# The prologue of a spectral mixing and ReGLU kernel in another order: x first on two queues, tables behind it, filters in halves, batch 1's stage A late

## The chip, the cores and the metric

The kernel runs on one core of a Trainium2 chip. The core has a matrix engine (TensorE, PE in the profile, its weight loads PEld), a vector engine (VectorE, DVE), a scalar engine (ScalarE, ACT), GpSimd (POOL) and a sync engine (SyncE, SP). Each of them takes its instructions strictly from its own list, and they wait for one another through semaphores. DMA transfers are issued from the lists of SP, ScalarE and GpSimd and are carried by 16 DMA engines that all of them share. The metric is the time of one execution on the device in microseconds (us); less is better.

## The reference, cut to what matters

Eight batches of 3008 tokens with 256 features are filtered in the frequency domain, and the result goes through a gated layer of width 1536.

```
x: (8, 3008, 256) float32     filt_r, filt_i: (1505, 256)
w_gate, w_val: (256, 1536)    w_out: (1536, 256)

X = rfft(x, axis=1);  Y = X * (filt_r + 1j * filt_i);  y = irfft(Y, n=3008, axis=1)
y = y.reshape(24064, 256)
out = (maximum(y @ w_gate, 0) * (y @ w_val)) @ w_out
```

## The kernel before, in words

The transform of length 3008 is split as 94 x 32 (`N1`, `N2`) and done with matrix products. For one batch the steps are these.

- **Stage A** multiplies x, with the 94 long axis on the partitions, by a cosine and sine table `WA`. x lies in two tiles `XF[0]` and `XF[1]`, 16 of the 32 positions of the short axis each. `load_x` fills them, a third of the rows per DMA, for column ranges given in units of `q`, a quarter of a tile.
- **Turning**: the result has to have the short axis on the partitions. For batch 0 two VectorE transposes do it in SBUF (`turn_a`, from the tiles `AS` to `AT`). For all other batches stage A's result is written to DRAM (`Abuf`) and read back in another order (`at`).
- **Forward transform** of the short axis with the table `F2` (`fwd`), **product** with the filter tiles `Ftr` and `Fti` (`product`), and **inverse transform** with `I2t` and `I2u` (`inv`). Six pieces i = 0 to 5 make a batch, each with eight matmuls, four products and sixteen matmuls. The result goes to DRAM (`Dbuf`) and is read back as `dC` (`load_d`).
- **Last inverse** (`item_c`, the table `M1`), which gives y transposed for a block of 512 tokens (`yT`).
- **The gated layer** (`gv` and `o_part`): 47 blocks of 12 steps. One step makes 128 columns of gate and value of a block (four matmuls, a ScalarE copy, a VectorE product) and a third of an output tile of the block before.

Batches 1 to 7 are transformed in between the steps of the gated layer; `at_step` holds which piece comes behind which step. Batch 1's `fwd` begins at step 16, that is the fifth step of the second block.

The order of the work is written by hand: each engine's list is the order in which the Python code emits instructions, and a DMA takes its place in the list of the engine that issues it. PSUM banks are handed out in rotation by `bank` and `done`. `hold_gpsimd` makes GpSimd wait for a tile, by copying eight columns of it, so that what it issues behind that comes later.

The change is in the **prologue**, all that stands ahead of the stream of the gated layer (lines 568 to 646), and in three helpers.

- `first_a(p, s, h)` is one item of batch 0's stage A: one matmul of 512 columns and a ScalarE copy. There are 16: p is a quarter of the 32 positions, s half of that quarter, h half of the features. p = 0 and s = 0 reads the first quarter of `XF[0]`.
- `items_a(1)` are the 16 items of batch 1's stage A. Items of c = 0 and 1 are copied mostly by ScalarE, those of c = 2 and 3 by VectorE; each fourth item completes a slab that SP writes to `Abuf`. `first_b(amid)` runs batch 0's six pieces, and calls `amid(i)` behind each piece, which may emit some of these items. Eight of the products of batch 0 run on GpSimd (`POOL_U`), from a copy `xs` that ScalarE makes; the other sixteen run on VectorE.
- `make_back_t` and `make_back_u` compute `I2t` and `I2u` on the chip from `F2` and a permutation in `tabs`; `place_own` copies the last groups and `M1` from `tabs`.
- `load_filters` loads the filters, on GpSimd's queue, for the rows 0 to 31 and 64 to 95. `place_filter(fi, a, half, copy)` copies them to the rows 32 to 63 and 96 to 127, for one half of the 24 groups (`H` = 12), with an engine's copy or with a DMA. Pieces 0 to 2 read the first half, pieces 3 to 5 the second.
- `load_vg` and `load_o` load the weights of the gated layer as bf16 (`WvT`, `WgT`, `WoT`), on GpSimd's queue.
- `warm(n)` emits n matmuls on a tile of ones, whose results are not used.

## Time and profile before

| | us |
|---|---|
| median of 3 runs | 891.37 |
| lowest and highest run | 888.9 and 892.23 |
| span of the profiled execution | 885.7 |
| the median above that span | 5.7 |
| TensorE busy | 872.1 (98%) |
| VectorE busy | 575.7 (65%) |
| ScalarE busy | 495.2 (56%) |
| GpSimd busy | 376.4 (43%) |

The profiled execution's own time is not listed apart from the three runs; what the profile has of it is the span, from the first to the last instruction.

The places in the prologue that the prediction uses, in us from the start of the span:

| | from | to |
|---|---|---|
| batch 0's stage A on TensorE | 7.63 | 22.4 |
| the two transposes on VectorE | 19.62 | 27.96 |
| batch 0's last product on GpSimd | 39.48 | 40.64 |
| the last write to `Dbuf` | 43.28 | 46.63 |
| the read of the first `dC` | 46.80 | 50.35 |
| the gated layer's first matmul | 52.32 | |
| the first matmul that reads `WoT` | 66.87 | |
| batch 1's first `fwd` | 73.14 | |

In the profile's lines a name such as L282 is a line of the kernel, and `psA<-XF,WA` means that psA is written from XF and WA. "xN" counts the instructions that were merged into the line. In brackets stands how long the engine idled ahead of them, and who ended that. SPq and ACTq are DMA issues on these engines' lists. The page's rows of digits show the span in 40 slices of 22 us each: a digit is the busy share in tenths. The chain of waits goes back from the last instruction, at each step to what released it.

### The profile page before, as it was taken

The numbers are of one execution on the slowest core, as the hardware profiler recorded it, in microseconds if no ns is written. First come the engines' busy times: TensorE is split into PE (matmuls) and PEld (weight loads), VectorE is DVE, ScalarE is ACT, GpSimd is POOL, SyncE is SP. The second block draws the span as 40 slices with busy tenths as digits, with TensorE's granted clock in tenths as the row PEclk, the third lists the DMA queues.
The fourth block names the chain that finished last, engine by engine and source line by source line (L and its number), as shares of the span: only waits on it lengthen the run. The fifth ranks groups of instructions, "written<-read, shape, count | busy, mean of one in ns | idle before, by whom it ended". The sixth has DMA issues, their size and how long they took to land.

```text
span 885.7 us, 19147 instructions
## 1 busy us (share of the span) xinstructions
PE 872.1 (98%) x7190; PEld 506.9 (57%) x7190; DVE 575.7 (65%) x875; ACT 495.2 (56%) x882; POOL 376.4 (43%) x375
## 2 busy tenths in 40 slices
PE   8989999999999999999999999999999999999997
PEld 3435655666555665556655665556655666666665
DVE  4866766676666676667765776657766577655553
ACT  5734555556555655556555556555655555555552
POOL 4654796147631667216780186803866000000001
PEclk9999999999999999999999999999999999999999
DMA  9994466533645337533376234663446512421111
GB/s 242 304 221 98 155 142 146 141 117 96 150 133 124 98 101 184 129 98 98 103 179 145 81 111 133 165 125 86 123 132 142 118 46 63 105 56 31 38 34 50
DMA packets 106067, 107.28 MB, mean 121 GB/s; under 512 B 20167, under 2 KB 90087, under 8 KB 105334
## 3 DMA queue, kind: packets, MB, share of 16 engines
q1 hardware_dynamic: 81286, 76.03, 33.5%
q0 software_dynamic: 23792, 29.16, 13.3%
q8 instruction: 57, 0.93, 0.4%
q10 hardware_dynamic: 896, 0.86, 0.3%
q14 instruction: 36, 0.29, 0.1%
HBM read 60.42 MB, written 48.23 MB: 123 GB/s over the span
## 4 chain that ended last, share of the span: by engine, by line
PE 92%; DMA 4%; DVE 1%; ACT 1%; issue 0%; POOL 0%; SPq 0%; ACTq 0%; DVEq 0%
PE psV L509 27%; PE psO L530 27%; PE psG L509 26%; PE psF L353 3%; PE psY L493 2%; PE psD L433 2%; PE psX L396 2%; DMA dC<-Dbuf 2%; DMA WoT<-in_moe_w_out_dram 1%; PE psA L282 1%; DVE AT L291 1%; PE psA L303 1%; PE psJ L565 0%; DMA Dbuf<-dsb 0%; DMA Dbuf<-AS 0%
## 5 line engine op out<-in xcount | busy, mean ns | idle before, releaser
L514 DVE SCALAR_TENSOR_TENSOR prod<-psG,vsb 128x512 bf16<-128x512 f32 x564 | 388.8, 690 | 262.4 <-ACT vsb L512 257.1
L512 ACT CAST vsb<-psV 128x512 bf16<-128x512 f32 x564 | 331.9, 589 | 266.5 <-PE psV L509 179.4
L509 PE MATMUL psV<-yT,WvT 128*128 128x512 bf16 x1128 | 337.6, 380 | 0.6 <-DVE yT L500 0.6
L530 PE MATMUL psO<-WoT,prod 128*128 128x256 bf16 x2256 | 336.7, 273 | 1.1 <-DMA WoT<-in_moe_w_out_dram 1.1
L509 PE MATMUL psG<-yT,WgT 128*128 128x512 bf16 x1128 | 335.8, 379 | 0.2 <-ACT yT L498 0.2
L530 PEld LDWEIGHTS <-prod 128*128 128x128 bf16 x2256 | 220.6, 98 | 144.8 <-issue 1.5
L509 PEld LDWEIGHTS <-WgT 128*128 128x128 bf16 x1128 | 110.1, 98 | 135.6 <-issue 2.5
L509 PEld LDWEIGHTS <-WvT 128*128 128x128 bf16 x1128 | 98.6, 98 | 41.3 <-issue 30.3
L274 POOL CAST scr<-prod 128x8 f32<-128x8 bf16 x24 | 4.5, 189 | 245.0 <-DVE prod L514 245.0
L554 POOL DMA_DIRECT2D out_dram<-osb x5 | 2.6, 536 | 195.7 <-ACT osb L543 195.7
L543 ACT COPY osb<-psO 128x512 f32<-128x512 f32 x92 | 53.9, 586 | 25.9 <-PE psO L530 23.5
L412 DVE TENSOR_TENSOR tt<-psX,Ftr 128x512 bf16<-128x512 f32 x96 | 65.0, 680 | 1.6 <-POOL uu L410 0.6
L339 POOL TENSOR_TENSOR fold<-XP 128x1024 f32<-128x1024 f32 x24 | 56.5, 2354 | 19.9 <-PE psF L353 18.8
L412 DVE TENSOR_TENSOR uu<-psX,Fti 128x512 bf16<-128x512 f32 x88 | 59.8, 680 | 0.0
L326 POOL DMA_DIRECT2D XP<-in_x_dram x96 | 57.6, 603 | 3.0 <-PE psG L509 1.6
L340 POOL TENSOR_TENSOR XP<-XP 128x1024 f32<-128x1024 f32 x24 | 56.3, 2348 | 2.0
L441 ACT CAST dsb<-psD 128x512 bf16<-128x512 f32 x94 | 50.6, 591 | 11.0 <-PE psD L433 11.0
L498 ACT CAST yT<-psY 128x512 bf16<-128x512 f32 x47 | 27.5, 586 | 31.0 <-PE psY L493 30.8
L360 DVE CAST asb<-psF 128x512 bf16<-128x512 f32 x48 | 30.9, 686 | 18.6 <-PE psF L353 18.6
L360 ACT CAST asb<-psF 128x512 bf16<-128x512 f32 x48 | 25.8, 589 | 30.5 <-PE psF L353 30.5
L493 PE MATMUL psY<-M,dC 96*128 96x94 bf16 (+18 forms) x604 | 37.7, 198 | 2.8 <-DMA dC<-Dbuf 2.8
L493 PEld LDWEIGHTS <-dC 96*128 96x128 bf16 x604 | 34.4, 97 | 7.2 <-DMA dC<-Dbuf 3.2
(80 smaller groups left out, 500.9 us busy)
## 6 DMA issues: line engine op xcount, KB each, us to landing
XP<-in_x_dram POOLq DMA_DIRECT2D x48, 256.0 KB, 5.8
Dbuf<-dsb SPq DMA_DIRECT2D x23, 512.0 KB
dC<-Dbuf SPq DMA_DIRECT2D x57, 192.0 KB
XP<-in_x_dram POOLq DMA_DIRECT2D x96, 96.0 KB, 2.6
Abuf<-asb SPq DMA_DIRECT2D x96, 96.0 KB
at<-Abuf SPq DMA_DIRECT2D x24, 384.0 KB
out_dram<-osb SPq DMA_DIRECT2D x69, 94.0 KB
XF<-in_x_dram SPq DMA_DIRECT2D x15, 256.0 KB
```

The source lines that it names most:

```text
L326: nc.gpsimd.dma_start(xp[r:r + 24, 0:4:2, :], _ap(x, (b * N1 * N2 + o) * D, [[N2 * D, 24], [47 * N2 * D, 2], [1, 512]]))
L339: tt(t, xp[:, 0:2], xp[:, 2:4], op=ALU.add)
L340: tt(xp[:, 2:4], xp[:, 0:2], xp[:, 2:4], op=ALU.subtract)
L360: copy(asf[:, :, q, :], banks[q])
L412: nc.vector.tensor_tensor(p, psX, filt, op=ALU.mult)
L441: copy(dsb[:, a, o:o + 2, :], psD[a])
L493: nc.tensor.matmul(psY[:, o:o + w], dCs[b, n2 // 8][:, n2 % 8, h * 128:(h + 1) * 128], M1[:, n1:n1 + w], start=True, stop=True)
L509: nc.tensor.matmul(pt[:, :W], w[:, h, ft * 128:(ft + 1) * 128], yt[:, h, :], start=(h == 0), stop=(h == 1))
L512: nc.scalar.copy(vsb, psV[:, :W])
L514: nc.vector.scalar_tensor_tensor(prod, in0=psG[:, :W], scalar=0.0, in1=vsb, op0=ALU.max, op1=ALU.mult)
L530: nc.tensor.matmul(psO[:, t % 2], prods[ft][:, t * 128:(t + 1) * 128], WoT[:, ft, :], start=(ft == 0), stop=(ft == NFT - 1))
L543: copy(osb[:, t0 % 2:t % 2 + 1], psO[:, t0 % 2:t % 2 + 1])
```

## The change

The prologue's instructions are put in another order and on other queues.

- x of batch 0 is loaded ahead of the tables, its first two quarters on the queues of SP and ScalarE in turn. The first quarter is loaded in four parts (the fourth fills the partitions that are otherwise zeroed), so that it needs no memset. `F2` and `tabs` come behind x, on SP.
- Stage A of batch 0 comes first on TensorE, all of it, and `make_back_t`, `make_back_u` behind it; the copies of `make_back_t` move from VectorE to ScalarE. `place_own` comes behind the transposes.
- The filters are loaded in two halves of the groups, 16 DMAs in place of 8, all behind the fourth piece of x. Three of the four copies of the first half and all of the second are DMAs of SP.
- Batch 1's x comes later on SP. Of the 16 items of batch 1's stage A, three are emitted within batch 0's pieces (before: eight), ten ahead of the first `item_c` and three behind it.
- The first half of the gate and value weights is loaded behind piece 3, the second half at once when the first `dC` is there; then the next `dC`, `WoT`, the other `dC`, and `at` last. Both DMAs of the first `dC` are issued by ScalarE.
- There are fewer warm-up matmuls ahead of the pieces, and two behind each of the pieces 0 to 3.

```diff
-    def load_x(b, eng, cols):
+    def load_x(b, engs, cols, ms=range(3)):
         w = NX2 * D
         for c, c0, c1 in cols:
-            for m in range(3):
+            for m in ms:
                 rows = min(32, B * N1 - (b * N1 + 32 * m))
-                eng.dma_start(XF[c][m:m + 4 * rows - 3:4, c0:c1],
+                engs[m % len(engs)].dma_start(XF[c][m:m + 4 * rows - 3:4, c0:c1],
...
         for e in range(2):
-            nc.vector.tensor_copy(I2t[:, 8 * q + e:8 * q + 8:2, :], psI[e])
+            nc.scalar.copy(I2t[:, 8 * q + e:8 * q + 8:2, :], psI[e])
...
     def load_filters():
-        for src, dst in FILT:
-            for a in range(2):
-                r, k1, n = a * 64, 1 + 24 * a, NG - 2 * a
-                nc.gpsimd.dma_start(dst[r:r + 31:2, 0:n, :], ...
-                yield
-                nc.gpsimd.dma_start(dst[r + 1:r + 32:2, 0:n, :], ...
+        for g0 in (0, H):
+            for src, dst in FILT:
+                for a in range(2):
+                    r, k1, n = a * 64, 1 + 24 * a + g0, H - (2 * a if g0 else 0)
+                    nc.gpsimd.dma_start(dst[r:r + 31:2, g0:g0 + n, :], ...
+                    nc.gpsimd.dma_start(dst[r + 1:r + 32:2, g0:g0 + n, :], ...
+            yield
...
     q = NX2 * D // 4
+    both, sp = (nc.sync, nc.scalar), (nc.sync,)
     nc.sync.dma_start(WA, ...)
-    nc.scalar.dma_start(F2, ...)
-    nc.scalar.dma_start(tabs, ...)
-    filters = load_filters()
-    next(filters)
-    nc.vector.memset(XF[0][:, 0:q], 0.0)
-    nc.gpsimd.memset(XF[0][:, q:2 * q], 0.0)
+    load_x(0, both, ((0, 0, q),), range(4))
     nc.vector.memset(junk, 1.0)
-    nc.vector.memset(XF[0][:, 2 * q:3 * q], 0.0)
-    nc.gpsimd.memset(XF[0][:, 3 * q:], 0.0)
+    nc.vector.memset(XF[0][:, q:2 * q], 0.0)
+    nc.gpsimd.memset(XF[0][:, 2 * q:], 0.0)
     nc.vector.memset(XF[1][:, 0:2 * q], 0.0)
     nc.gpsimd.memset(XF[1][:, 2 * q:], 0.0)
-    load_x(0, nc.sync, ((0, 0, q), (0, q, 2 * q), (0, 2 * q, 4 * q), (1, 0, 2 * q), (1, 2 * q, 4 * q)))
+    load_x(0, both, ((0, q, 2 * q),))
+    load_x(0, sp, ((0, 2 * q, 4 * q), (1, 0, 2 * q), (1, 2 * q, 4 * q)))
+    nc.sync.dma_start(F2, ...)
+    nc.sync.dma_start(tabs, ...)
     for (src, dst) in FILT:
         nc.vector.memset(dst[64:128, NG - 2:, :], 0.0)
+    filters = load_filters()
+    hold_gpsimd(XF[1][:, 2 * q - 8:2 * q])
+    next(filters)
     load_own_filters()
-    hold_gpsimd(XF[0][:, 4 * q - 8:4 * q])
-    for _ in filters:
-        pass
-    warm(8)
+    next(filters)
+    warm(6)
+    for p, s, h in [(p, s, h) for p in range(2) for s in range(2) for h in range(2)]:
+        first_a(p, s, h)
+    for p, h in ((2, 0), (3, 0), (2, 1), (3, 1)):
+        for s in range(2):
+            first_a(p, s, h)
     for i in range(3):
         make_back_t(i)
-    warm(3)
-    for s in range(2):
-        for h in range(2):
-            first_a(0, s, h)
     for i in range(3):
         make_back_u(i)
-    for p, h in ((1, 0), (1, 1), (2, 0), (3, 0), (2, 1), (3, 1)):
-        for s in range(2):
-            first_a(p, s, h)
-    place_own()
     for h in range(2):
         turn_a(h)
-    for i in range(12):
+    place_own()
+    for i in range(6):
         warm(2)
     place_filter(1, 0, 0, nc.gpsimd.tensor_copy)
-    place_filter(1, 1, 0, nc.scalar.copy)
-    for half, cols in ((0, ((0, 0, 2 * q),)), (1, ((0, 2 * q, 4 * q),))):
+    for a in range(2):
+        place_filter(0, a, 0, nc.sync.dma_start)
+    place_filter(1, 1, 0, nc.sync.dma_start)
+    load_x(1, sp, ((0, 0, 2 * q),))
+    for fi in range(2):
         for a in range(2):
-            place_filter(0, a, half, nc.sync.dma_start)
-        load_x(1, nc.sync, cols)
-    for a in range(2):
-        place_filter(1, a, 1, nc.sync.dma_start)
-    load_x(1, nc.sync, ((1, 0, 4 * q),))
-    nc.sync.dma_start(WF, ...)
+            place_filter(fi, a, 1, nc.sync.dma_start)
+    load_x(1, sp, ((0, 2 * q, 4 * q),))
     early = items_a(1)
     def amid(i):
         if i == 3:
             place_nyq()
-        if i == 0:
-            warm(4, 256)
-        for _ in range((0, 1, 1, 2, 2, 2, 0)[i]):
+            load_vg(0, DFF // 2)
+        if i == 3:
+            load_x(1, sp, ((1, 0, 4 * q),))
+        if i < 4:
+            warm(2)
+        for _ in range((0, 0, 0, 0, 1, 1, 1)[i]):
             next(early)()
-    hold_gpsimd(AT[0:32, NG - 1, D - 8:])
-    load_vg(0, DFF // 2)
     first_b(amid)
-    load_d(0, 0, 1, (nc.sync, nc.scalar))
+    load_d(0, 0, 1, (nc.scalar, nc.scalar))
     hold_gpsimd(dCs[0, 0][:, 7, D - 8:])
-    load_vg(DFF // 2, 3 * DFF // 4)
+    load_vg(DFF // 2, DFF)
     load_d(0, 1, 2, (nc.gpsimd, nc.gpsimd))
-    load_vg(3 * DFF // 4, DFF)
+    load_o()
+    load_d(0, 2, 4, (nc.gpsimd, nc.gpsimd))
+    nc.sync.dma_start(WF, ...)
     for i, f in enumerate(early):
         f()
-        if i == 6:
+        if i == 9:
             for h in range(2):
                 item_c(0, h)
-    for c in range(2):
+    for c in range(4):
         load_at(1, c)
-    hold_gpsimd(yTs[0][:, 0, 0:8])
-    load_o()
-    for c in range(2, 4):
-        load_at(1, c)
-    load_d(0, 2, 4, (nc.gpsimd, nc.gpsimd))
```

More of the change, by code (lines that the diff above doesn't have):

```diff
@@ L231, in load_filters @@
     def load_filters():
-        for src, dst in FILT:
-            for a in range(2):
-                r, k1, n = a * 64, 1 + 24 * a, NG - 2 * a
-                nc.gpsimd.dma_start(dst[r:r + 31:2, 0:n, :],
-                                    _ap(src, k1 * D, [[N1 * D, 16], [1, n * D]]))
-                yield
-                nc.gpsimd.dma_start(dst[r + 1:r + 32:2, 0:n, :],
-                                    _ap(src, (N1 - k1) * D, [[N1 * D, 16], [-D, n], [1, D]]))
+        for g0 in (0, H):
+            for src, dst in FILT:
+                for a in range(2):
+                    r, k1, n = a * 64, 1 + 24 * a + g0, H - (2 * a if g0 else 0)
+                    nc.gpsimd.dma_start(dst[r:r + 31:2, g0:g0 + n, :],
+                                        _ap(src, k1 * D, [[N1 * D, 16], [1, n * D]]))
+                    nc.gpsimd.dma_start(dst[r + 1:r + 32:2, g0:g0 + n, :],
+                                        _ap(src, (N1 - k1) * D, [[N1 * D, 16], [-D, n], [1, D]]))
+            yield
     def load_own_filters():
@@ L568 @@
     q = NX2 * D // 4
+    both, sp = (nc.sync, nc.scalar), (nc.sync,)
     nc.sync.dma_start(WA, nc.inline_tensor(wa_h, name="dft_wa").ap())
-    nc.scalar.dma_start(F2, nc.inline_tensor(f2_h, name="dft_f2").ap())
-    nc.scalar.dma_start(tabs, nc.inline_tensor(tab_h, name="dft_tab").ap())
-    filters = load_filters()
-    next(filters)
-    nc.vector.memset(XF[0][:, 0:q], 0.0)
-    nc.gpsimd.memset(XF[0][:, q:2 * q], 0.0)
+    load_x(0, both, ((0, 0, q),), range(4))
     nc.vector.memset(junk, 1.0)
-    nc.vector.memset(XF[0][:, 2 * q:3 * q], 0.0)
@@ L578 @@
-    nc.gpsimd.memset(XF[0][:, 3 * q:], 0.0)
+    nc.vector.memset(XF[0][:, q:2 * q], 0.0)
+    nc.gpsimd.memset(XF[0][:, 2 * q:], 0.0)
     nc.vector.memset(XF[1][:, 0:2 * q], 0.0)
     nc.gpsimd.memset(XF[1][:, 2 * q:], 0.0)
-    load_x(0, nc.sync, ((0, 0, q), (0, q, 2 * q), (0, 2 * q, 4 * q), (1, 0, 2 * q), (1, 2 * q, 4 * q)))
+    load_x(0, both, ((0, q, 2 * q),))
+    load_x(0, sp, ((0, 2 * q, 4 * q), (1, 0, 2 * q), (1, 2 * q, 4 * q)))
+    nc.sync.dma_start(F2, nc.inline_tensor(f2_h, name="dft_f2").ap())
@@ L582 @@
+    nc.sync.dma_start(tabs, nc.inline_tensor(tab_h, name="dft_tab").ap())
     for (src, dst) in FILT:
         nc.vector.memset(dst[64:128, NG - 2:, :], 0.0)
+    filters = load_filters()
+    hold_gpsimd(XF[1][:, 2 * q - 8:2 * q])
+    next(filters)
     load_own_filters()
-    hold_gpsimd(XF[0][:, 4 * q - 8:4 * q])
-    for _ in filters:
-        pass
-    warm(8)
+    next(filters)
+    warm(6)
+    for p, s, h in [(p, s, h) for p in range(2) for s in range(2) for h in range(2)]:
+        first_a(p, s, h)
@@ L605 @@
+    for i in range(6):
         warm(2)
     place_filter(1, 0, 0, nc.gpsimd.tensor_copy)
-    place_filter(1, 1, 0, nc.scalar.copy)
-    for half, cols in ((0, ((0, 0, 2 * q),)), (1, ((0, 2 * q, 4 * q),))):
-        for a in range(2):
-            place_filter(0, a, half, nc.sync.dma_start)
-        load_x(1, nc.sync, cols)
-    for a in range(2):
-        place_filter(1, a, 1, nc.sync.dma_start)
-    load_x(1, nc.sync, ((1, 0, 4 * q),))
-    nc.sync.dma_start(WF, nc.inline_tensor(fold_h, name="dft_fold").ap())
+    for a in range(2):
+        place_filter(0, a, 0, nc.sync.dma_start)
@@ L621, in amid @@
             place_nyq()
-        if i == 0:
-            warm(4, 256)
-        for _ in range((0, 1, 1, 2, 2, 2, 0)[i]):
+            load_vg(0, DFF // 2)
[4 more added lines that the diff above has]
+        for _ in range((0, 0, 0, 0, 1, 1, 1)[i]):
             next(early)()
-    hold_gpsimd(AT[0:32, NG - 1, D - 8:])
-    load_vg(0, DFF // 2)
     first_b(amid)
-    load_d(0, 0, 1, (nc.sync, nc.scalar))
+    load_d(0, 0, 1, (nc.scalar, nc.scalar))
     hold_gpsimd(dCs[0, 0][:, 7, D - 8:])
-    load_vg(DFF // 2, 3 * DFF // 4)
+    load_vg(DFF // 2, DFF)
     load_d(0, 1, 2, (nc.gpsimd, nc.gpsimd))
-    load_vg(3 * DFF // 4, DFF)
+    load_o()
+    load_d(0, 2, 4, (nc.gpsimd, nc.gpsimd))
+    nc.sync.dma_start(WF, nc.inline_tensor(fold_h, name="dft_fold").ap())
     for i, f in enumerate(early):
         f()
-        if i == 6:
+        if i == 9:
             for h in range(2):
                 item_c(0, h)
-    for c in range(2):
+    for c in range(4):
         load_at(1, c)
-    hold_gpsimd(yTs[0][:, 0, 0:8])
-    load_o()
-    for c in range(2, 4):
-        load_at(1, c)
-    load_d(0, 2, 4, (nc.gpsimd, nc.gpsimd))
     prologue.close()
```

## The prediction

> **What bounds the kernel now.** I read the page first, for the whole span.
>
> ```profile
> span 885.7 us, 19147 instructions
> ...
> PE   8989999999999999999999999999999999999997
> ...
> DMA  9994466533645337533376234663446512421111
> ```
>
> TensorE is busy nearly throughout; from the fourth slice on (about 73 us) only work taken off it would pay, and the change takes none off there. What it can win lies in the first three slices, where the DMA engines are full too. So next the chain of waits over the first 75 us, with the steps that carry it.
>
> ```profile
> 2.53 3.60 PE psJ L565 x8
> ...
> 7.79 3.43 PE psA L282 x8
> ...
> 11.88 7.10 PE psA L282 x16
> ...
> 19.62 3.50 DVE AT L291
> ...
> 23.78 4.19 DVE AT L291
> ...
> 43.28 3.35 DMA Dbuf<-AS
> ...
> 46.80 3.55 DMA dC<-Dbuf
> ...
> 52.53 0.85 PE psV L509 x2
> ...
> 57.47 11.43 DMA WoT<-in_moe_w_out_dram
> ...
> 73.21 0.34 PE psX L396 x8
> ```
>
> Each line is start, length, what. Batch 0 goes: warm-up matmuls, stage A (psA), two transposes on VectorE (AT), products and inverse until 43.28, a write to DRAM, the read back (dC), then the gate/value stream (psV). The stream waits once for WoT. The psX at 73.14 in TensorE's timeline (batch 1's first transform, step 16 of the stream) is my finish line: behind it both kernels do the same.
>
> Then the timelines of TensorE, GpSimd and SP, for what each step costs and what it waits for.
>
> ```profile
> 22.23 5.34 PE L565 MATMUL psJ<-junk 128*128 128x512 bf16 x24
> ...
> 41.90 6.25 PE L303 MATMUL psA<-XF,WA 128*96 128x512 f32 x14
> 50.49 0.62 PE L493 MATMUL psY<-M,dC 96*128 96x94 bf16 x12 [2.35 <-DMA dC<-Dbuf]
> ```
>
> ```profile
> 29.77 6.73 POOL L410 TENSOR_TENSOR uu<-xs,Fti 128x512 bf16<-128x512 f32 x6
> 36.57 0.39 POOL L258 COPY Ftr<-nyq 1x256 bf16<-1x256 bf16 x1
> ```
>
> ```profile
> 1.96 10.16 SPq L190 DMA_DIRECT2D XF<-in_x_dram  x15
> ```
>
> Seven batch-1 items cover the trip through DRAM until 48.14, then TensorE idles 2.35 us; and the first matmul pairs of the stream take 0.85 us where later ones take 0.43. Last, the DMA queues between 30 and 43 us:
>
> ```profile
> DMA packets 1504, 4.15 MB, mean 319 GB/s; under 512 B 178, under 2 KB 818, under 8 KB 1395
> ```
>
> That is the rate a full mix of x loads, weights and writes reaches here.
>
> **The change, part by part.**
>
> *Start.* The junk memset leads on VectorE (0.48, ends 1.50 instead of 2.47), and six warm-ups of 3.60/8 = 0.45 end at 4.26. psA then needs the weight table and the first quarter of x: five DMAs on two queues (SP's x issue costs 10.16/15 = 0.68) are issued by 2.5; between the 2.2 us to landing of the 16 KB filter row and the page's 2.6 for a 96 KB x load they are in at 4.0 to 4.9. I take 4.3 for the first psA, against 7.79. The make_back work (0.90 + 0.65 on the chain) is out of the way. But the first warm-ups run at 0.45, the 24 later ones at 5.34/24 = 0.22, and the slow stretch lasted from 2.53 to about 7.0, 4.5 us. Begun at 1.56 it ends at 6.1, so 1.8 us of stage A run at half speed: 0.9 lost; bounds 0 (it ends at 4.3) and 2.1 (it lasts to 8.5, psA's half speed being all of the excess).
> [...]
> From first psA to the twelfth copy the trace has 19.60 − 7.79 = 11.81, less 0.65 of make_back: 11.16. AT starts at 4.3 + 11.16 + 0.9 = 16.4 and ends 8.35 later at 24.7 instead of 27.97: 3.3 gained.
>
> *x in time?* Fifteen x loads at 0.64 to 0.68 on SP would be as slow as before; four of the first seven stay on SP, so the last is issued at 9.4 instead of 12.1, and stage A wants it at 12.9. Free. The extra fourth part (128 KB) and the late tables (wanted by make_back at 19, issued at 10) hide under stage A. [...]
>
> *make_back behind stage A.* Six psI copies move to ScalarE: 0.35 each (VectorE's 2.08/6) to 0.59 (ScalarE's 128x512): 2.1 to 3.5, plus 1.57 for I2u, behind the last AS copy at 19.6: done at 23.3 to 24.7, under the transposes. Without that cover each us would delay the first inverse. place_own (3 × 0.19) now stands ahead of VectorE's first product, which idled 0.50 there for psX: 0.1. Warm-up matmuls removed and added fill waits: free.
>
> *Filters.* GpSimd is held until the fourth chunk of x lands (some 10.5, before 11.81), then issues 16 + 4 DMAs at 0.48 to 0.61: until 21.5. Its Fti copy (2.73), queued behind, ends at 24.3, ahead of its first product at 24.7 + 1.1 = 25.8. SP's three copies of half 0 land before that too. The second half goes through 20 to 27, its copies are issued to 27.5; nothing shows how long SP's copies take, the loads in the same crowd took 5.1 to 6.9, so 32. VectorE wants them at 30.4, GpSimd at 31.7: some 0 to 2 us, mostly under GpSimd's chain; I take 0.
>
> *Products.* Batch 1's items leave this stage (8 before, 3 now), so TensorE is not full here. But GpSimd is: 6.73 for six products, 0.75 for the Nyquist rows, two weight loads now in the middle (0.73 + 0.71), two products at 1.15: 12.0 from 25.8 is 37.8 less overlaps of the copies, say 37.2. Before, the last ended at 40.64, 12.67 after AT; now 12.5. The lighter TensorE buys almost nothing. Inverse and copy take 1.1 to 2.6 (40.64 to 43.28 before, an item's copy in the way); I take 1.6: the last Dbuf write is issued at 38.8 instead of 43.28, 4.5 earlier.
>
> *The write and the read back.* Here the gain is lost again. In before the last x load (28.75) and the first weights (28.26) were through at about 41 and the final write met a free DMA. Now x waits on SP behind the first Dbuf write: that came 7.5 after AT, now at most, so 31.6 to 32.2; the weights follow at 33.5. From 33 on there stand 1.57 MB of Dbuf, 1.57 of x, 0.79 of weights: 3.93 MB at 319 GB/s = 12.3 us, that is 45.3. Bounds: the write overtakes (38.8 + 3.35 = 42.1), or it comes all last with its own latency (47). I take 45.2, nearest to the rate of the same mix, against 46.63. dC now has both issues on ScalarE, one 0.34 after the other, then 3.69: psY at 49.3, before 50.49. Behind the waiting issues ScalarE holds four psA copies; TensorE needs the first of those banks only for the last item before psY, so this adds 0 to 0.5, inside the wait for dC.
> Ten items (0.893 each) now end at 37.7 + 8.9 = 46.6: TensorE still idles some 2.7 us. Behind psY come 0.62 and three items, 2.7: the stream starts at 52.6, before 52.32.
>
> *The stream to the finish line.* Before: 73.14 − 52.32 = 20.8. Clean it would be 17 gate/value steps of 0.865, five outputs of 0.435 and 0.5 of psY: 17.4. Lost are 1.2 to half speed in the first pairs, 1.4 to the two waits for WoT, 0.8 to small waits. WoT is now issued at 52.6 behind weights and one dC (1.97 MB with itself; the queue ran 4.7 MB in 19.4 us from 52.2 on): about 61, wanted at 64: the 1.4 goes. Late next is at: now last of 4.7 MB, 51 + 19.4 = 70.4, wanted at 70.8 to 72. The half speed stays if 2.7 us idle act as 2.35 did; 0 to 1.7 in all, half in my sum. So the finish line: 52.6 + 20.8 − 1.4 − 0.5 = 71.5, a gain of 1.6. The fold table (64 KB, first wanted past 140 us) is off the path.
>
> **Sum.** 885.7 − 1.6 = 884.1 of span. The median of the runs lies 5.7 above the profiled span (the lowest run 3.2), which I carry over: 889.8.
>
> **Rivals.**
> A, *no collision* (25 in 100). The last write gets through by 42.1 because the engines serve SP's queue ahead of GpSimd's. Then psY is bound by the ten items at 46.6, no idle, no half speed: stream at 49.9, finish line 49.9 + 20.8 − 2.6 = 68.1, 5.0 gained, or 3 if at is then late by 2: 886.4 to 888.4, and 885 if the slow start costs nothing. For it: separate queues, and x (SP) is issued ahead of the weights. Against: the DMA engines are busy nearly without a break from 30 to 43.
> B, *slower: the second filter half is late* (15 in 100). The eight small loads may cost as much each as the large ones (seven landed about 1.0 apart, 17 to 22.4, by GpSimd's wait at 21.71). Then half 1 lands at 30 to 32, its copies at 36, and GpSimd's sixth product waits from 31.7: 4 to 5 us straight down the chain to the dC read, 893 to 896. It decides from about 33.5; beyond 38 the kernel is slower by more than 0.5%.
> C, *at is the new stall* (included in the forecast's upper end). at stands last now; if it lands at 73 instead of 70.4 the whole gain goes: 891 to 892.
>
> **How the numbers follow.** Forecast (collision as summed, with C) 60 in 100, its own range 887.5 to 892; A 25, B 15. About 0.5% (4.5 us) is what a measurement of this kernel can tell from no change. Faster than 886.9 is 17 of A's 25, and 7 of the forecast's 60 for bounds that all fall well: 0.24. Slower than 895.8 is the far half of B, 8, and 6 of the forecast where C costs more than its price: 0.14. Within: 0.62. The range takes in A's middle and B's middle: 885.5 to 894.5.
>
> **What would show it.** First psA near 4.3 and at half speed for a while; AT done at 24 to 25.5; GpSimd's last product near 37; the final Dbuf write issued near 39 but landing after 44; TensorE idle for dC again; no wait for WoT, perhaps one for at. I am wrong upward if the write lands at 42 and the stream starts at 50; wrong downward if products wait for Ftr or Fti copies near 31.

## The result and the profile after

| | median, us | runs | lowest and highest |
|---|---|---|---|
| before | 890.37 | 4 | 888.9 to 892.23 |
| after | 900.15 | 4 | 898.09 to 901.15 |

The ratio is 1.0102, with a 95% interval of 1.008 to 1.0124. The change makes the kernel 1.0% slower, 9.8 us; the prediction was 1.6 us faster. The profiled execution of after took 901.15, with a span of 899.4; against the span of before (885.7, an execution at the lower end) that is 13.7 more. The marks that are compared below stand in both in the same order, so the place where the time is lost can be read; the size is that of the medians.

These are the page's span and rows of digits after (40 slices of 22.5 us), and the row of the granted clock before.

```profile
span 899.4 us, 19131 instructions
...
PE   8788999999999999999999999999999999999997
...
PEclk9889999999999999999999999999999999999999
DMA  8897448443465344663355433753346512231111
```

```profile
PEclk9999999999999999999999999999999999999999
```

Nearly all that differs lies in the first four slices: TensorE's digits fall to 7 and 8, and the granted clock to 8. At the gated layer's products 11.9 of the 13.7 have come by 95 us; the other 1.9 are two later waits of TensorE, 1.51 for `dC` at 148.88 (before 0.45) and 0.55 for `at` at 188.51. Next the chain of waits after, from 5 to 84 us, the answer to the chain shown in the prediction (start, length, what).

```profile
5.16 12.37 PE psA L283 x24
...
18.17 3.47 DVE AT L292
...
22.33 4.22 DVE AT L292
26.59 6.91 DMA Ftr<-Ftr
...
34.01 2.57 DMA Fti<-Fti
...
46.40 0.51 SPq L445
...
47.69 6.08 DMA Abuf<-asb
53.81 3.27 DMA dC<-Dbuf
...
57.66 7.21 DMA WvT<-in_moe_w_val_dram
...
74.54 8.65 DMA at<-Abuf
...
83.32 0.41 PE psX L397 x8
```

Three transfers stand here that were not in the chain before: a filter copy (`Ftr<-Ftr`, `Fti<-Fti`), the weights `WvT`, and `at`. The write of batch 0 was there with 3.35 and has become a slow stretch up to 53.8: the profile names `Abuf<-asb`, which landed at 53.77, but the `dC` issue began at 53.40, right behind the last `Dbuf` write's landing at 53.30. The finish line (batch 1's first psX) moves from 73.14 to 83.32, 10.2 later. TensorE's timeline says what each costs there; the brackets hold the idle time ahead and who ended it.

```profile
37.45 0.42 PE L434 MATMUL psD<-tt,I2t 64*64 64x256 bf16 x2 [4.26 <-DVE uu L413]
...
57.21 1.01 PE L494 MATMUL psY<-M,dC 96*128 96x94 bf16 x12 [1.15 <-DMA dC<-Dbuf]
58.05 5.42 PE L304 MATMUL psA<-XF,WA 128*96 128x512 f32 x6
...
83.32 0.41 PE L397 MATMUL psX<-at,F 64*64 64x256 bf16 x8 [2.07 <-DMA at<-Abuf]
```

VectorE's product (`uu`) is named ahead of the first, but VectorE itself waited there, for the copies: two gaps of 2.13 and 2.39 in its own timeline.

```profile
33.63 0.69 DVE L413 TENSOR_TENSOR tt<-psX,Ftr 128x512 bf16<-128x512 f32 x1 [2.13 <-DMA Ftr<-Ftr]
36.70 0.69 DVE L413 TENSOR_TENSOR uu<-psX,Fti 128x512 bf16<-128x512 f32 x1 [2.39 <-DMA Fti<-Fti]
```

Around or right behind these idle times the granted clock falls to half (36.13 to 42.95, 56.61 to 63.44 and 83.92 to 87.33). The three items behind psY took 5.42 in place of 2.7.

Split at the same events, the 10.2 are: −1.4 until the transposes end (26.55 against 27.97); +4.5 from there to the issue of the last `Dbuf` write (19.85 against 15.31); +3.6 from that issue to psY (10.81 against 7.21: the write took 6.90 to land, before 3.35); +4.2 from psY to the stream's first matmul (6.05 against 1.83); −0.8 in the stream up to the finish line.

One view holds the cause of the middle parts. Here are busy times by stretches of 12 us (stretch, length, busy time of PE, PEld, DVE, ACT and POOL with counts, then granted clock, DMA share, GB/s), before and then after.

```profile
24.00:36.00 12.00, 11.38 (x109) 4.72 (x111) 11.07 (x13) 8.88 (x13) 8.29 (x10) 1.00 1.04 298
36.00:48.00 12.00, 12.00 (x94) 4.87 (x86) 8.84 (x14) 6.69 (x13) 3.55 (x5) 1.00 0.79 257
```

```profile
24.00:36.00 12.00, 7.80 (x93) 3.11 (x91) 8.14 (x12) 6.46 (x13) 8.51 (x7) 1.00 0.76 171
36.00:48.00 12.00, 10.55 (x82) 4.27 (x83) 7.03 (x11) 5.51 (x10) 5.64 (x7) 0.72 0.95 287
```

From 24 to 36 us, where the kernel before filled the DMA engines (298 GB/s), the changed one moves 171. The rows show two reasons: the engines were busy for less of the time (a share of 0.76 against 1.04; the profile's shares can pass 1), and while busy they moved less (171/0.76 = 225 against 298/1.04 = 287). At the end of that stretch the loads were not slow for want of bandwidth: they had not been issued. SP's waits say why (line, releaser, total, times, longest): 17 us of waiting for filter loads, with batch 1's x queued behind them, where before it was 6.8. After, and then before:

```profile
SPq L255 <- DMA Ftr<-in_filt_r_dram: 8.8, 4, 6.2
SPq L255 <- DMA Fti<-in_filt_i_dram: 8.2, 3, 5.6
```

```profile
SPq L254 <- DMA Ftr<-in_filt_r_dram: 6.8, 2, 5.7
```

By 36 us 7.65 MB have passed instead of 9.48. What is missing then is moved later, on top of the `Dbuf` writes that batch 0's way out needs.

From this comes the theory that I tested: the prologue is bound by the DMA engines, and the change loses time because loads are issued later, behind waits on SP's and GpSimd's lists, so that the engines are partly idle up to 36 us and full of other bytes when the last `Dbuf` write, the first `dC` and `at` need them (theory D). Its rivals: the late second filter half is the loss by itself (theory H in its later form), or the new start and the late items of batch 1 are.

### The profile page after: what moved, and what is told of

Its sections match the earlier page's. It is cut to its first block, busy times and chain, and to the rows that moved or that the text cites. A ratio compares the mean times of both kernels' runs of the same rounds, so it can differ in the third digit from the quotient of the medians.

```text
span 899.4 us, 19131 instructions
## 1 busy us (share of the span) xinstructions
PE 877.4 (98%) x7177; PEld 508.6 (57%) x7177; DVE 573.0 (64%) x868; ACT 495.3 (55%) x887; POOL 379.0 (42%) x378
## 4 chain that ended last, share of the span: by engine, by line
PE 88%; DMA 7%; DVE 1%; issue 1%; SPq 1%; POOL 1%; ACT 0%; DVEq 0%; POOLq 0%; ACTq 0%
PE psV L510 26%; PE psO L531 26%; PE psG L510 25%; PE psF L354 3%; PE psD L434 2%; PE psY L494 2%; DMA at<-Abuf 2%; PE psX L397 2%; DMA dC<-Dbuf 2%; PE psA L283 1%; DVE AT L292 1%; DMA WvT<-in_moe_w_val_dram 1%; DMA Ftr<-Ftr 1%; DMA Abuf<-asb 1%; PE psA L304 1%
```

## The experiments

There are fifteen experiments. The table has their times and four places of each profiled execution: megabytes moved by 36 us, issue and landing of the last `Dbuf` write, the first psY, the finish line. One execution can differ from its median (that of e9 took 890.58, 1.8 above, that of e1 even 902.72, 4.0 above), so the places of single executions are not to be compared to less than 2 us, and those of e1 to less than 4; the ratio is to the runs of before made beside it.

| | median | ratio, 95% interval | MB by 36 | last write | psY | finish |
|---|---|---|---|---|---|---|
| before | 889.9 to 890.7 | 1 | 9.48 | 43.28 to 46.63 | 50.49 | 73.14 |
| after | 900.15 | 1.0102, 1.008 to 1.0124 | 7.65 | 46.40 to 53.30 | 57.21 | 83.32 |
| e1 x behind the filter copies | 898.68 | 1.0100, 1.0068 to 1.0132 | 7.79 | 43.54 to 52.59 | 56.36 | 83.80 |
| e2 weights early | 896.16 | 1.0064, 1.0043 to 1.0085 | 8.38 | 46.88 to 49.23 | 54.68 | 78.87 |
| e3 at ahead of dC | 895.68 | 1.0056, 1.0035 to 1.0078 | 7.80 | 46.10 to 52.63 | 56.56 | 80.40 |
| e5 e2 and e3 | 893.75 | 1.0038, 1.0022 to 1.0054 | 8.49 | 48.62 to 50.97 | 56.42 | 78.58 |
| e6 e1, e2 and e3 | 891.62 | 1.0021, 1.0003 to 1.0038 | 8.37 | 45.76 to 48.15 | 53.56 | 76.48 |
| e12 filters whole | 897.15 | 1.0080, 1.0059 to 1.0101 | 8.11 | 44.95 to 50.19 | 54.10 | 80.68 |
| e13 e6 and filters whole | 892.12 | 1.0024, 1.0012 to 1.0036 | 7.89 | 46.86 to 49.21 | 54.66 | 77.37 |
| e4 before and new start | 890.09 | 0.9995, 0.998 to 1.001 | 9.66 | 44.43 to 46.93 | 51.02 | 73.32 |
| e7 e4, 12 warm-ups fewer | 888.64 | 0.9984, 0.9968 to 1.0001 | 9.67 | 43.69 to 46.43 | 50.01 | 72.22 |
| e8 before and more bytes | 893.44 | 1.0042, 1.0024 to 1.006 | 9.24 | 45.46 to 52.05 | 55.72 | 79.62 |
| e9 e7 and items late | 888.74 | 0.9982, 0.9967 to 0.9997 | 9.54 | 45.51 to 47.87 | 53.31 | 75.16 |
| e10 e7 and halved filters | 895.27 | 1.0050, 1.0031 to 1.007 | 8.58 | 50.10 to 52.60 | 56.54 | 79.34 |
| e11 e7 and dC on GpSimd | 889.75 | 1.0002, 0.9986 to 1.0018 | 9.62 | 43.35 to 46.65 | 51.70 | 72.53 |
| e14 e9 and late part | 890.42 | 1.0000, 0.9991 to 1.001 | 9.42 | 44.57 to 46.91 | 52.37 | 74.24 |
| e15 e13 without late part | 891.93 | 1.0019, 1.0007 to 1.003 | 7.93 | 45.60 to 49.10 | 53.41 | 76.89 |

### Taking the changed kernel back, one load at a time

**e1**: batch 1's first x load goes behind the copies of the second filter half.

```diff
-    load_x(1, sp, ((0, 0, 2 * q),))
     for fi in range(2):
         for a in range(2):
             place_filter(fi, a, 1, nc.sync.dma_start)
-    load_x(1, sp, ((0, 2 * q, 4 * q),))
+    load_x(1, sp, ((0, 0, 2 * q), (0, 2 * q, 4 * q)))
```

> The changed kernel, but batch 1's first x load (768 KB) stands on SP behind the four copies of the second filter half instead of ahead of them. Theory F (in the changed kernel this x load, in 8 KB packets, shares the DMA engines with the second half of the filters, in 512 B packets, and starves it: the last filter load, issued at 24.1, lands at 33.9): the last filter load lands near 28, its copy near 31, VectorE and GpSimd wait 0 to 1 us where they waited 4.5 and 3.0, the last write of batch 0 is issued at 42 to 43 instead of 46.4, and the kernel takes 3 to 5 us less, about 896. Rival S (the sixteen small filter loads are slow by themselves, whatever runs beside them): the last filter load still lands past 32, the waits stay, 900. Rival T (the end of the prologue is set by the DMA queue of GpSimd alone, whatever stands ahead): the write comes earlier but batch 1's transform starts within 1 us of 83.3.

The last filter load landed at 30.4 instead of 33.9, the last write was issued 2.9 earlier; it landed only 0.7 earlier, and nothing was left of it at the finish line. x had delayed the filters, but making them earlier only moved the wait to the writes and to `at`:

```profile
83.80 0.64 PE L397 MATMUL psX<-at,F 64*64 64x256 bf16 x8 [3.50 <-DMA at<-Abuf]
```

Part of e1's gain was lost ahead of the products already. VectorE's small copy to `I2t` took 2.55 there (after: 0.40), up to the end of GpSimd's filter copy at 28.24, and the first product came at 29.44 instead of 27.19.

**e2**: the first half of the weights goes back to where it was, behind the transposes.

```diff
     def amid(i):
         if i == 3:
             place_nyq()
-            load_vg(0, DFF // 2)
...
+    hold_gpsimd(AT[0:32, NG - 1, D - 8:])
+    load_vg(0, DFF // 2)
     first_b(amid)
```

> The changed kernel, but the first half of the gate and value weights is issued ahead of batch 0's pieces, as before the change, and not behind the fourth. Theory C (the weights, issued at 38.6, share the engines with the four writes of batch 0; the last write, issued at 46.4, lands only at 53.3): the last write lands 3 to 4 us after its issue instead of 6.9, and the stream starts about 3 us earlier relative to that issue. If theory F holds as well, the 0.79 MB now compete with the second filter half and cost there what they gain later: 898 to 901, with the products waiting 5 to 7 us. Rival (the last write is late because x of batch 1 stands ahead of it on SP's own queue): it still takes 6 us or more to land.

The weights now use the idle time in 28 to 36 us, and the last write lands 2.35 after its issue, not 6.90: 3.4 us faster by the ratios. The wait for the filter copies stays (3.27 in TensorE's timeline), and `at` is still late by 3.19.

**e3**: the four reads of `at` stand ahead of the last two `dC`.

```diff
-    load_d(0, 2, 4, (nc.gpsimd, nc.gpsimd))
...
     for c in range(4):
         load_at(1, c)
+    load_d(0, 2, 4, (nc.gpsimd, nc.gpsimd))
```

> The changed kernel, but batch 1's at is read ahead of the last four dC loads and not behind them. Theory T (from the landing of the first dC on GpSimd's DMA queue is the bound: 4.3 MB at 180 to 190 GB/s, and at stands last in it, landing 26 us after the first dC): at lands 4 us earlier, TensorE does not wait 2.1 us for it nor run 3.4 us at half speed behind that wait, 3 to 4 us less: 896.5. Rival (at waits for its own source, the write of Abuf, not for its place): nothing changes within 1 us.

Some 4 us faster (4.6 thousandths). TensorE no longer waits for `at`, and the third stretch at half speed (83.92 to 87.33) goes too; more than the 2.07 of the wait came back.

**e5** joins e2 and e3, **e6** joins all three.

> The changed kernel with two parts undone together: the first half of the gate and value weights ahead of batch 0's pieces, and at read ahead of the last four dC loads. One by one these gave 4.0 and 4.5 us. Theory D (the DMA engines are the bound of the prologue: some 18.5 MB have to pass ahead of batch 1's transform, in the changed kernel 7.6 MB have passed at 36 us where 9.2 had before; what is issued later, or queued ahead of what is needed, delays it): the stream still starts near 57.8, at lands near 75.5 and TensorE has no wait for it, batch 1's transform starts at 75.5 to 76.5 instead of 83.3, the kernel takes 891.5 to 893.5. Rival (the two gains are the same wait seen twice): no better than 895.

> The changed kernel with three parts undone: those two, and batch 1's first x load behind the second filter half. That third one by itself brought the last write of batch 0 2.9 us forward in issue but only 0.7 in landing. Theory D and C: with the weights out of the way of the writes the 2.9 us now reach the landing too; stream at 55, batch 1's transform at 73 to 74, time 889 to 891, as before the change. Rival (the halved filter loads cost by themselves, more DMAs and more waits): the products still wait 2 us or more and the time stays at 892 or above.

(The 9.2 MB at 36 us that are named for the kernel before are 9.48 by the queues' total, as in the table.)

The savings of e1, e2 and e3 were 0.2, 3.8 and 4.6 in thousandths of the time (differences of the ratios: 1.0102 − 1.0100, and so on), together 8.6; e6 saves 8.1. Four fifths of the loss is thus in the place of three loads. e1, worth nothing alone, is worth 1.7 by the medians once the writes are free (e5 to e6, whose intervals overlap).

**e12** undoes the halving of the filter loads alone, **e13** does so on top of e6.

```diff
-        for g0 in (0, H):
-            for src, dst in FILT:
-                for a in range(2):
-                    r, k1, n = a * 64, 1 + 24 * a + g0, H - (2 * a if g0 else 0)
+        for src, dst in FILT:
+            for a in range(2):
+                r, k1, n = a * 64, 1 + 24 * a, NG - 2 * a
```

> The changed kernel with the halving of the filter loads alone undone: the eight whole loads of before, behind the change's hold on the fourth piece of x and ahead of the four small own loads; copies, x, weights and the rest as in the change. Theory H (the halving is the main cost: e10 was 0.66% slower than e7 by it alone): all filter loads are issued by 17 and land by 25, the copies of the second half land by 31, no vector engine waits long for them, the last Dbuf write is issued 3 to 5 us earlier than 46.4; about 5 us faster than the change, 893 to 896. Theory D in its strict form (the late bytes of x and weights bind in any case): the last write is issued earlier, but lands at 51 to 53 as in e1, and the time stays at 898 to 900.

> The kernel with the three loads moved (e6_all_three) and the filter loads whole: what is left of the change is the new start, the filters behind a hold one piece of x later, their copies on SP, batch 1's items late, and the order of the weights. Theory H: halving was the rest of the loss, so the time falls by 2 to 5 us from e6's 891.6 to 887 to 889.6, about e7's or below, with no wait of TensorE for a filter product and no half speed in the prologue or one stretch at most. Rival (the three moves already removed what halving costs, and the rest lies in the late weights and at): 890.5 to 892.

Theory H, that the halving is the main cost, falls here: e12 saves 2.2 thousandths by the medians (the intervals of after and e12 overlap), e13 nothing over e6. In e12 the last copies landed by 36.1, hardly earlier than after's 36.6. The later hold, x and the copies are the same in both, and I put it down to them; that was not tried apart. TensorE then waits for the next things in it:

```profile
66.03 0.61 PE L509 MATMUL psG<-yT,WgT 128*128 128x512 bf16 x2 [2.36 <-DMA WgT<-in_moe_w_gate_dram]
...
80.68 0.41 PE L396 MATMUL psX<-at,F 64*64 64x256 bf16 x8 [2.35 <-DMA at<-Abuf]
```

### Building up from the kernel before

**e4** is the kernel before with the new start alone: x first on two queues, the tables behind it, stage A first, `make_back` behind it with its copies on ScalarE. The filters are whole, all behind the hold on the third piece of x; there are 24 warm-ups ahead of the pieces, as before. **e7** has 12 of them.

```diff
+    load_x(0, both, ((0, 0, q),), range(4))
...
+    load_x(0, both, ((0, q, 2 * q),))
+    load_x(0, sp, ((0, 2 * q, 4 * q), (1, 0, 2 * q), (1, 2 * q, 4 * q)))
...
+    filters = load_filters()
     load_own_filters()
     hold_gpsimd(XF[0][:, 4 * q - 8:4 * q])
     for _ in filters:
         pass
...
-    for i in range(12):                  # e7 only
+    for i in range(6):
         warm(2)
```

> The kernel before, with only the new start: x first on two queues, tables behind it, stage A of batch 0 first, the six copies on ScalarE, the table placement behind the transposes. Filters are loaded whole, held behind the third piece of x as before (without the one early load), and all that follows the warm-up ahead of the pieces is as before. Theory: the transposes end at 26.5 instead of 28.0, as in the changed kernel, and the start by itself gains 0 to 1.5 us: 889 to 890.5, the filter loads, with the early one gone, being the next bound (the ScalarE copy of Fti ended at 27.75 before). Rival (the new start costs by itself, because the filters come later): first product past 29, 891 to 894.

> The kernel before with the new start alone, but 12 instead of 24 warm-up matmuls ahead of the pieces: with 24 they ended at 29.2, 2.2 us after the transposes, and TensorE held the first transform back. A path of dependent work as the bound: the first transform starts at 27 instead of 29.2, and the gain of some 1.5 to 2 us arrives: 888 to 888.6. Theory D (the DMA engines are the bound already before the change): the earlier write is taken back by waits for weights, WoT or dC, 889.3 to 890.3, no different from before.

In e4 the transposes end at 26.95, but TensorE's list still holds the warm-ups until 29.3, so its first psX comes at 29.21, later than before (28.01). That is read from TensorE's timeline of e4:

```profile
23.94 5.34 PE L565 MATMUL psJ<-junk 128*128 128x512 bf16 x23
```

With half of them (e7) psX starts at 27.21. The start is then worth 0.16%, about 1.4 us by the median, with an interval that reaches from 2.8 to nothing; in the profiled executions the transposes end 1.0 (e4) and 0.8 (e7) earlier than before. Warm-ups that filled a wait cost nothing until the wait got shorter.

**e8** is the kernel before with two copies of weight rows, 0.79 MB each, from DRAM to DRAM, which nobody reads, behind the fold table on SP.

```diff
+    extra = [dram.tile([128, DFF], FP32, name=f"extra{i}") for i in range(2)]
...
+    for i in range(2):
+        nc.sync.dma_start(extra[i], _ap(moe_w_gate, i * 128 * DFF, [[DFF, 128], [1, DFF]]))
     early = items_a(1)
```

> The kernel before with two more DMA transfers and nothing else: SP copies 1.57 MB of the gate weights from DRAM to a DRAM buffer that nobody reads, issued behind the fold table at about 31 us, where SP has nothing to issue for 4 us. Theory D: these bytes take about 4 us of the sixteen engines, some 1 to 2 of which fit into the gap at 46 to 49; the last write lands later, batch 1's transform starts 2 to 4 us later, 892 to 894.5. Rival (the prologue is bound by the chain of engines and single latencies, DMA volume beside it is hidden): within 0.8 us of before.

The kernel gets 0.42% slower, 3.7 us. In the profiled execution the last write is issued 2.2 later (1.2 of it was there before the copies were issued: the transposes end at 29.19, before at 27.96) and takes 6.6 to land, as in the changed kernel, though no filter, copy or weight has moved. The copies stand ahead of the write on SP's own queue, so e8 by itself can't tell a full queue from full engines; e2, where weights on GpSimd's queue are what moves, shows that loads of another queue delay the write too. This is the disputed cost by itself, in TensorE's timeline:

```profile
55.72 1.04 PE L494 MATMUL psY<-M,dC 96*128 96x94 bf16 x12 [5.70 <-DMA dC<-Dbuf]
```

**e9** adds the change's places for batch 1's items to e7, **e10** adds the halved filter loads to e7, **e11** gives both reads of the first `dC` to GpSimd in e7, without the hold behind them.

```diff
-        for _ in range((0, 1, 1, 2, 2, 2, 0)[i]):     # e9
+        if i < 4:
+            warm(2)
+        for _ in range((0, 0, 0, 0, 1, 1, 1)[i]):
...
-        if i == 6:                                    # e9
+        if i == 9:
             for h in range(2):
                 item_c(0, h)
...
-        for src, dst in FILT:                         # e10
+        for g0 in (0, H):
+            for src, dst in FILT:
...
+            yield
...
-    load_own_filters()
     hold_gpsimd(XF[0][:, 4 * q - 8:4 * q])
-    for _ in filters:
-        pass
+    next(filters)
+    load_own_filters()
+    next(filters)
...
-    load_d(0, 0, 1, (nc.sync, nc.scalar))             # e11
-    hold_gpsimd(dCs[0, 0][:, 7, D - 8:])
+    load_d(0, 0, 1, (nc.gpsimd, nc.gpsimd))
```

> The kernel with the new start and 12 warm-ups (e7_start_12_warmups), plus the change's placing of batch 1's stage A: none of its 16 items behind pieces 0 to 3, one each behind the last three calls, ten ahead of the first item_c, three behind it, and two warm-ups behind each of pieces 0 to 3. Loads and queues are left as they are. Theory D (the DMA engines bound the prologue, the place of the items only moves TensorE's own work): before the last Dbuf write nothing is gained, since the vector engines and the loads set its time (issued 43 to 44); behind it ten items of 0.89 in place of seven hold TensorE 2.7 longer than the 2.1 it now waits for dC, so the stream starts 0.5 to 1 later, and so do the weights' and Abuf's users: 0 to 1.5 us slower than e7, that is 888.5 to 890.5. Rival (the lighter TensorE lets batch 0's pieces run faster): the last write is issued 1 to 2 us earlier than 43.7 and the time falls to 886.5 to 888.

> The kernel with the new start and 12 warm-ups (e7_start_12_warmups), plus the filters loaded in halves: 16 loads in place of 8 behind the same hold on x's third chunk, the first half of the groups first; copies, weights and batch 1's x as in e7. Theory D, in its narrow form (the second filter half is late only because it stands behind a later hold, four loads more, and x): eight more issues of about 0.55 us keep GpSimd's list 4.4 us longer, so GpSimd's own Fti copy starts near 24 in place of 20 and its first product 1 to 2 later; the second half lands 1 to 4 later than in e7; batch 0's last product 1 to 3 later: 889 to 892. Rival (halves help, since the first products need only half of the bytes): the first product starts earlier than in e7 and the time is 886.5 to 888.6.

> The kernel with the new start and 12 warm-ups (e7_start_12_warmups), with both reads of the first dC issued by GpSimd and no hold on dC behind them, so that the other weights follow the read on the same queue instead of waiting 3.5 us for it to land. In e7 the DMA engines moved little from 44 to 53 us. Theory D: weights, dC, WoT and at all land 2 to 3.5 us earlier; the waits of TensorE for WgT (0.8) and WoT (1.5) go; the dC read itself lands 0 to 1 us later (two issues of 0.65 one behind the other on one queue): 1 to 2.5 us faster than e7, 886 to 887.6. Rival (the weights' packets take the read's place on the engines, as they took the last write's): dC lands 2 us later or more, TensorE drops to half speed there, and the time is 888.6 to 891.

The place of the items makes no difference (0.9982 against 0.9984). The halving, behind the earlier hold and with all else as in e7 except that the four own loads now stand between the halves, costs 6.6 thousandths, 6 us and more than was expected. Its second half is issued at 19.7 to 23.8 on GpSimd, behind the four own loads, for two of which GpSimd had to wait 2.10 and 1.08 (in e7 the whole loads are issued at 10.5 to 14.8). The traces of before and after show what such waits are for: the program's DMAs on GpSimd's list tell their landing through eight semaphores in turn, and of 352 with one eight places ahead of them none is issued until 0.28 after that one has landed (ten at just 0.28). In e10 it is the ninth and the tenth DMA that waited, for the landing of two loads of the first half; the eight loads of e7 were issued without a wait. So the last copies on SP come 3 us later, beside x and the weights, and land at 39.31 (e7: 34.74). VectorE's timeline has it:

```profile
39.43 0.69 DVE L413 TENSOR_TENSOR uu<-psX,Fti 128x512 bf16<-128x512 f32 x1 [5.72 <-DMA Fti<-Fti]
```

So one part of the change costs 0.66% where it is the main delay, and 0.22% or nothing where other loads are late too: the costs don't add up, they stand behind each other. e11 went as its rival had it: the weights' loads are issued 1.7 earlier, but the `dC` reads land at 51.56 (e7: 49.97), TensorE idles 3.48 and the matmuls behind that are slow (psY takes 1.01, in e7 0.63).

**e14** and **e15** split what is left between e9 (0.9982) and e13 (1.0024). e14 is e9 with the change's order behind the pieces (both `dC` issues on ScalarE, the second half of the weights at once, WoT, `at`, `dC`). e15 is e13 with the order of before there, so that it keeps the later hold, the copies on SP and x behind all copies. The edit of e14 to e9, which e15 takes back from e13 (the fold table, 64 KB, moves with it):

```diff
-    load_d(0, 0, 1, (nc.sync, nc.scalar))
+    load_d(0, 0, 1, (nc.scalar, nc.scalar))
     hold_gpsimd(dCs[0, 0][:, 7, D - 8:])
-    load_vg(DFF // 2, 3 * DFF // 4)
+    load_vg(DFF // 2, DFF)
     load_d(0, 1, 2, (nc.gpsimd, nc.gpsimd))
-    load_vg(3 * DFF // 4, DFF)
+    load_o()
...
-    for c in range(2):
-        load_at(1, c)
-    hold_gpsimd(yTs[0][:, 0, 0:8])
-    load_o()
-    for c in range(2, 4):
+    for c in range(4):
         load_at(1, c)
     load_d(0, 2, 4, (nc.gpsimd, nc.gpsimd))
```

> e9_items_late (0.9982 of before) plus the change's order of everything behind batch 0's pieces, with at ahead of the later dC as in e13: both dC issues on ScalarE, then the whole second half of the weights, dC, WoT, at, dC, and the fold table behind the first dC. Filters and x are as in e9. If this late part carries the 0.4% by which e13 is slower than e9, its time is 891 to 892.5. If the early part carries it (filters behind a later hold, the copies on SP, x behind all copies: 1.65 MB fewer bytes by 36 us in e13), it stays at 888 to 889.5.

> e13_three_and_filters_whole (1.0024 of before) with everything behind batch 0's pieces in the order of before (as in e9), the fold table behind the third piece of x: it keeps e13's filters behind the later hold, the own filter rows behind them, the copies on SP, and x of batch 1 behind all copies. If the early part carries the 0.4%, its time is 891 to 892.5; if the late part does, 888 to 889.5. Together with e14 the two parts can add up, 890 each.

Early part 3.7 thousandths, late part 1.8, with intervals of 1 to 1.5 on each side of the ratios: the early part carries most of it, the late one some or little. The DMA queues' totals up to 36 us, of e15 and of e14, have the same mark as after and before:

```profile
DMA packets 3876, 7.93 MB, mean 220 GB/s; under 512 B 671, under 2 KB 2898, under 8 KB 3474
```

```profile
DMA packets 3957, 9.42 MB, mean 262 GB/s; under 512 B 748, under 2 KB 2822, under 8 KB 3366
```

Over the whole table, the kernels that had moved at least 9.4 MB by then lie within 0.2% of before (e8 apart, whose bytes are extra), and those with 8.6 MB or less are 0.2 to 1% slower. Within the second group the order of what follows decides (e2, e3), and the mark is a poor scale: e13 and e15 with 7.9 MB are 0.2% slower, e2 and e10 with 8.4 and 8.6 are 0.6 and 0.5%. Nor do few bytes always mean idle engines: from 24 to 36 us those of e10 were about as busy as before (7 to 9 tenths in every slice of 0.9 us, before 8 or 9) and moved 224 GB/s. That bytes missing by 36 us are the cause is thus shown for e8 and e2, and argued for the rest.

The fastest of all is e9 or e7, 0.2% under before; e9's interval just excludes no change, e7's just doesn't. No kernel tried was clearly better than that.

## Why the prediction was wrong

- *Start.* psA came at 5.16, not 4.3: TensorE waited 0.96 for x's first quarter, whose parts landed at up to 5.0 (the prediction's own bounds were 4.0 to 4.9). Half speed lasted until about 8.7, not 6.1 (ScalarE's copies of stage A come 1.71 apart up to 8.95 and 0.87 apart from there). AT ended at 26.55: 1.4 gained of 3.3. Right in kind, the sizes just past the bad end of their bounds. That such a gain reaches the total fits e7's median, but its interval doesn't exclude that nothing does.
- *x in time, make_back, WoT, warm-ups costing nothing.* No wait for the later pieces of x, none of `I2u`, none for WoT any more: right. The six psI copies left 0.9 of small waits on TensorE (0.6 the longest), ahead of the warm-ups, so off the path.
- *Filters, "I take 0".* This is the first step that failed. GpSimd's hold ended at 12.24, not 10.5. The last load of the second half was issued at 23.59, not by 21.5, and landed at 33.87, not 27; the last SP copies, each of which waits for its load, were issued at 32.79 and 34.01, not by 27.5, and landed at 36.6, not 32. The prediction gave the last small load 5.5 us to land; by the trace it (80 KB) needed 10.3, with three x loads of 256 KB issued 0.5 to 1.7 ahead of it. In place of 0 the products waited, VectorE 2.13 and 2.39 and GpSimd 3.01, and from the transposes' end to the last write's issue went 19.85 instead of 15.31. Rival B was this place, at 15 in 100 and with 4 to 5 us; e10 prices the halving at 6 where nothing else is late.
- *Products.* With the filters late, the last product ended at 42.94, not 37.2, and the last write was issued at 46.40, not 38.8. The chain of GpSimd's own work was no longer what counted. (Its terms make 11.2, not the 12.0 of the sum; by them the 37.2 would be 37.0.)
- *The write and the read back, "45.2".* The collision was forecast and it came, later and larger. The prediction let the engines run at 319 GB/s from 33 us on, and didn't ask what they would have moved up to there: by 36 us 1.83 MB less than before, while SP waited for filters. At the 319 GB/s that the prediction used, these are 5.7 us. The write landed at 53.30, and e2 (weights out of its way) and e8 (extra bytes in its way, in the kernel before) show that the bytes ahead of it are what it waits for.
- *ScalarE's wait for dC, "0 to 0.5".* ScalarE waited at its `dC` issue until 53.4, and TensorE idled 1.46 at 54.97 for a psA copy queued behind it. Within the next idle time, the 1.15 for `dC`, the clock fell to half (at 56.61, until 63.44), and the three items behind psY took 5.42 in place of the 2.7 of the sum.
- *at, "Late next is at".* Rival C: it landed at 83.19, not 70.4, and cost 2.07, plus 3.4 us at half speed behind it. The prediction counted the bytes of GpSimd's queue from one issue time on; by the trace the eight semaphores held the list up, 1.75 and 2.06 ahead of the last two `dC` and 1.94 and 1.71 among the four `at`, which were issued at 68.74 to 74.54. e3, which only exchanges `at` and the last `dC`, gains 4.1. The place was right; it was priced at no more than the gain of 1.6, since neither these waits nor the half speed were counted.

The mistake behind several of these is one: each load was given a landing time from its own issue and a rate, and the waits on SP's and GpSimd's lists, which decide when the next ones are issued, were taken as free as long as nobody needed that load yet. What stays open: how the early part's share of the last 0.4% divides (hold, copies on SP, x) was not tried, nor why one copy of 192 KB took 2.57 and another 6.91 (34.01 and 26.59 in after), beyond the crowd it is in.

## What to carry to other kernels

Where a prologue is bound by DMA engines, count the bytes that have passed by a certain time, before and after the change, not only the landing of each load: a stretch in which an issuing queue waits for one load is lost for all that stand behind it (here SP's 17 us of waiting for filter loads, with batch 1's x queued behind them). Count the DMAs as well: here a load cut in two took two of the eight places that GpSimd's list had under way at once (waits of 2.10 and 1.08 in e10). When loads are reordered, ask of each wait on an issuing engine what is queued behind it, and undo several moves together before concluding that one of them was harmless: e1 alone showed nothing, and the halving (with the own loads between) cost 6 us or none, depending on what else was late. Fillers such as warm-up matmuls have to be cut as the wait that they fill gets shorter.

## What the runs showed of the hardware

- TensorE's clock dropped after idle times that were rather short. In before it idled 2.35 at 48.14 and the clock was at half from 51.41 for 3.41 us; in e11, behind 3.48 of idle, psY took 1.01 and the next two psA matmuls 2.00. After 1.73 (e4) and 1.45 (e7) at the same place they took 0.64 and 0.63, and 1.08 in both. But the length of one idle time doesn't decide: after 2.36 of idle ahead of 66.03 in e12 the gate and value pairs kept their 0.6, and in e3, behind two of 1.09 and 1.18 with two matmuls between them, psY took 0.93 and the next six psA 4.16 (e12: 0.62 and 2.79). In before and after, the four stretches at half speed between 12 and 100 us are 3.41 long or twice that (one in before, three in after), and in after they begin and end whole multiples of 3.41 apart (36.13, 42.95, 56.61, 63.44, 83.92, 87.33). In the 3.41 us ahead of each of the four, TensorE idled 2.34 (before), 2.94, 2.00 and 2.07 (after) in all; of the other stretches at full speed, counted in the same steps from 12 to 100 us, none has more than 0.92.
- The small filter loads were slower with large transfers beside them. The four that were issued between 22.1 and 23.6 in after needed 7.3 to 10.3 us to land with x beside them (from 24 to 36 us 96 of 929 packets had 8 KB or more, and 664 less than 2 KB). The last two of these, of 80 KB, needed 10.2 in the median; in e1, without x, 5.6.
- 1.57 MB of copies in e8 cost 3.7 us by the ratio. In the profiled execution the last write landed 5.4 later, of which 1.2 were there before the copies were issued.
- VectorE's copy to `I2t` (0.19 in e4, e12 and e13) ended within 0.1 us of GpSimd's 2.73 us filter copy in after and e1, where the two met: it took 0.40 in after (to 26.97, the filter copy to 26.91) and 2.55 in e1 (to 28.29, the filter copy to 28.24). The transposes of VectorE ran beside the same copy as without it, at 4.21 to 4.25 in after, where only the second met it.
